# Two attention blocks on one core: A's V weights on another queue, their loads behind a VectorE copy, and the exps of phi(K) planned apart

## The chip, the cores and the metric

The kernel runs on one core of a Trainium2 chip. The core has five engines that run their own instruction streams and wait for each other on semaphores: TensorE (PE, matrix products into the PSUM banks), VectorE (DVE), ScalarE (ACT, exp and copies), GpSimd (POOL) and SyncE (SP, which only issues transfers). ACT and POOL issue transfers too, each on a queue of its own. The metric is the device time of one launch in microseconds; lower is better.

## The reference

Two independent blocks over 2048 positions and width 512, with 32 heads of 16; their results stand side by side in the output.

Block A (segments of 512 positions, with a memory that is carried along):

```python
phi = lambda t: where(t > 0, t + 1.0, exp(t))
for s in range(4):                      # segments of 512
    p = softmax(qs @ ks.T * scale + causal_mask)
    a_dot = p @ vs
    a_mem = (phi(qs) @ M) / (phi(qs) @ z + 1e-6)
    o = g * a_mem + (1 - g) * a_dot     # g = sigmoid(beta), one per head
    M += phi(ks).T @ vs;  z += phi(ks).sum()
out_a = concat(o) @ wo
```

Block B is plain attention of all 2048 queries over all 2048 keys, from one weight `wqkv`, followed by its own `wo`. All inputs are bf16.

## The kernel before

**Units.** The work is cut into units: one block of 512 queries and one group of four heads (`hg`, 0 to 7). A has 4 segments with 8 units each, B has 4 query blocks with 8 units each. The list begins with six units of A's first segment; from then on B's units stand, with A's others spread between them. For each unit PE makes scores with the keys on the partitions, ACT turns them into exps (L702 and L699 for A, L766 for B; called `pT`), and PE multiplies these with V into an accumulator `acc` (L924). A unit of A has five score tiles: widths of 1280 and 1024 alternate, and the last has 512. In A, POOL clears the masked triangle of each `pT` (L713) before PE may use it. B's exps are shared between ACT and DVE, which computes some of them with integer operations (L818, L784). A finished accumulator is transposed by DVE (L855), its row sums inverted (L858), and scaled by POOL (`rw` and `tN`, L872 and L876).

**Banks.** Scores lie in two tiles of PSUM, of three and two banks, used in turn. There are two further banks, `d_ps`, for everything else: projections (L334), DVE's scores (L807), memory and output products. There is one accumulator.

**Order.** The order of all instructions is written when the program is built, by a planner inside the kernel: a loop keeps a model time `c["t"]` and modelled times of ACT, DVE and POOL, and at each step issues scores, a batch of products with V, or a *chore*. A chore is a projection of K, Q or V, a transposition or an output product. Chores are sorted by due time and start once their condition holds, among others a model time at which their weights or inputs are taken to be there (`WA_AT`, `XB_AT`, `WB_AT`). `at(time, f)` puts an action off to a model time. On the chip each engine then runs its own instructions strictly in this order. Where the planner sees PE without work it puts filler products with zeros into the accumulator (L907).

**The front.** Four tiles of A's x and the first 128 columns of A's K and Q weights are loaded first (L75 to L78, SP and ACT). PE transposes x (L312); the halves are copied by ACT and by DVE (L953). Right behind ACT's copy stand, in the code, the loads of A's remaining weights (`load_rest_a`, L168 to L170). Then come the first Q and K projection, the two query masks by DVE (L963 and L967), B's loads on SP (`load_b`, L175 to L188), the K copy by ACT (L965) and the planner's loop. `setup_gates` (L143 to L154) makes the gates of A's memory, an exp on ACT, four small operations on DVE and ten on POOL. The later query tiles are masked by POOL (L353).

**phi(K).** For each of the four groups of 128 columns of A's K, SP transposes the finished keys (L399); later `more` (L401) makes exp on ACT into a tile `ek` that exists twice (L403), and three operations on POOL (L405 to L407). The time at which `more` is placed is not before `PHI_AT`.

Of the kernel before, what the change touches and what calls it, by code (L numbers as in the profile page):

```python
# [19 lines left out]
P = 128  # L20
# [21 lines left out]
def fast_path(ctx, tc, nc, A_x, A_wq, A_wk, A_wv, A_wo, A_beta, B_x, B_wqkv, B_wo, out, flag):  # L42
# [19 lines left out]
    def wview(w):  # L62
        return w.rearrange("(cc p) n -> p cc n", p=P)
    wq_a = const.tile([P, 4, D], BF16, name="wq_a")
    wk_a = const.tile([P, 4, D], BF16, name="wk_a")
    wv_a = const.tile([P, 4, D], BF16, name="wv_a")
# [18 lines left out]
    n = 1  # L85
# [41 lines left out]
    for j in range(4):  # L127
        nc.gpsimd.dma_start(out=beta_t[32 * j:32 * j + 32, :].rearrange("p (r t) -> p r t", t=2),
                            in_=bv[j].partition_broadcast(32))
# [35 lines left out]

    def load_rest_a():

        nc.scalar.dma_start(out=wv_a[:], in_=wview(A_wv))  # L168
        nc.scalar.dma_start(out=wk_a[:, :, P:], in_=wview(A_wk)[:, :, P:])
        nc.scalar.dma_start(out=wq_a[:, :, P:], in_=wview(A_wq)[:, :, P:])  # L170

# [15 lines left out]
        nc.sync.dma_start(out=wo_a[:], in_=wview(A_wo))  # L187
        nc.sync.dma_start(out=wo_b[:], in_=wview(B_wo))  # L188

    WA_AT = dict(v=6500, k=8500, q=10000)  # L190
    XB_AT, WB_AT = (10000, 18000, 23500, 28000), dict(k=13500, v=16000, q=21000)
    PHI_AT = 31000


# [37 lines left out]
    c = dict(t=0.0, act=0.0, dve=0.0, gp=0.0, mode=None)  # L232
# [37 lines left out]
    def act_cost(n):  # L270
        return 100.0 + 0.833 * n
# [8 lines left out]
    def gp_do(n, ready, rate=1.05):  # L280
        c["gp"] = max(c["gp"], ready) + 100.0 + rate * n
        return c["gp"]

    def act_do(ns, ready):
        c["act"] = max(c["act"], ready) + ns
        return c["act"]
# [4 lines left out]
    def at(time, fn):  # L291
        lcount[0] += 1
        heapq.heappush(later, (time, lcount[0], fn))
# [11 lines left out]
    def d_bank(dtype=F32):  # L305
        bank = d_next.pop() if d_next else ps_d.tile([P, 512], F32, name="d_ps", tag="d")
        return bank[:] if dtype == F32 else bank[:].bitcast(dtype)

    def fill_xT(bank, sbs):
        for n, i in enumerate(sbs):  # L310
            for cc in range(4):
                nc.tensor.transpose(bank[:, (4 * n + cc) * P:(4 * n + cc + 1) * P],  # L312
                                    xtiles[i][:, cc * P:(cc + 1) * P], ident[:])
        pe(60.0 * 4 * len(sbs), "full")
# [81 lines left out]
    def phi_k(s, rt):  # L396

        kn = phik_t[(s, rt)] = sb_.tile([P, 4, P], BF16, name="phik", tag="xin", bufs=4)
        nc.sync.dma_start_transpose(out=kn[:], in_=KT_at[(s, rt)][:])  # L399

        def more():  # L401
            e = sb_.tile([P, 4, P], BF16, name="ek", tag="e", bufs=2)
            nc.scalar.activation(e[:], kn[:], ACT.Exp)  # L403
            act_do(act_cost(512) + 100, c["t"])
            nc.gpsimd.tensor_scalar(e[:], e[:], 1.0, 0.0, ALU.min, ALU.max)  # L405
            nc.gpsimd.tensor_scalar(kn[:], kn[:], 3e38, 0.0, ALU.min, ALU.max)
            nc.gpsimd.tensor_tensor(kn[:], kn[:], e[:], op=ALU.add)  # L407
            gp_do(1024, c["act"] + LAT)
            gp_do(512, 0, 2.1)
            phik_at[s] = c["gp"] + LAT  # L410
            phik_n[s] = phik_n.get(s, 0) + 1
        at(max(c["dve"] + 12000, PHI_AT), more)

    def chore_k(k, s, rt):
        def evac(bank):
            uses(k, s)
            nc.vector.tensor_copy(k_dst(k, s, rt), bank)
            d_done(dve_do(dve_cost(512), c["t"] + LAT))
            k_ready[(k, s, rt)] = c["dve"] + LAT
            if k == "a" and s < NSEG - 1:  # L420
                phi_k(s, rt)
        d_job(lambda b, ccs: proj(b, ccs, weights(k, "k"), rsl(rt), xT_tile(k, s)), evac)
# [15 lines left out]
    def chore_q(k, s, rt):  # L438
        def evac(bank):
            uses(k, s)  # L440
            qc = sb_.tile([P, 512], BF16, name="qc", tag="qc", bufs=3)
            if k == "a":
                nc.vector.tensor_copy(qc[:], bank)
            else:
                nc.vector.tensor_scalar(qc[:], bank, QSCALE, None, ALU.mult)  # L445
            d_done(dve_do(dve_cost(512), c["t"] + LAT))
            q_masks(k, s, rt, qc)
            if k == "a" and s > 0:
                at(c["dve"] + 400, lambda: phi_q(s, rt, qc))
        d_job(lambda b, ccs: proj(b, ccs, weights(k, "q"), rsl(rt), xT_tile(k, s)), evac)  # L450
# [5 lines left out]
    def chore_v(k, i):  # L456
        def evac(bank):
            uses(k, i // 4)
            nc.vector.tensor_copy(v_dst(k, i), bank.rearrange("p (h d) -> p h d", d=DH))
            d_done(dve_do(dve_cost(512), c["t"] + LAT))  # L460
            v_ready[(k, i)] = c["dve"] + LAT
        d_job(lambda b, ccs: proj(b, ccs, weights(k, "v"), slice(0, D), xT_tile(k, i // 4), i % 4), evac)
# [79 lines left out]
    def chore(need, fn, ok=None, due=None, am=None):  # L542
        chores.append(dict(due=due, need=need, fn=fn, ok=ok, n=len(chores), am=am))

    def q_free(k, cc, rt):

        g = 4 * cc + rt - QTB[k]
        return g < 0 or exhausted(U[uidx[(k, g // 4, 2 * (g % 4) + 1)]])
# [5 lines left out]
    def begin(k, cc, hg):  # L554
        return U[uidx[(k, cc, hg)]]["at"]
# [5 lines left out]
    for i in range(4):  # L561
        chore(begin("a", 0, 0) + 4000 + 500 * i, lambda i=i: chore_v("a", i), ok=lambda: scount[0] >= 5 and now() >= WA_AT["v"])
    for rt in range(1, 4):
        n = begin("a", 0, 2 * rt)
        chore(n - 3000, lambda rt=rt: chore_k("a", 0, rt), ok=lambda rt=rt: now() >= WA_AT["k"] and q_free("a", 0, rt))
        chore(n - 4500, lambda rt=rt: chore_q("a", 0, rt), ok=lambda rt=rt: now() >= WA_AT["q"] and q_free("a", 0, rt))
    for g in range(4):
        n = b0 + 5500 * g
# [5 lines left out]
    for rt in range(1, 4):  # L574
        n = begin("b", 0, 2 * rt)
# [7 lines left out]
    for s in range(1, NSEG):  # L583
        n = begin("a", s, 0)
# [22 lines left out]
    n = 1e18  # L607
    for x in chores[::-1]:
        n = x["due"] = min(x["need"], n - (1200 if x["need"] < b0 + 35000 else 2500))
# [45 lines left out]
    def s_tile(dtype=F32):  # L655
        n = scount[0] % 2
        scount[0] += 1
        c["t"] = max(c["t"], sfree[n])
        return n, ps_s.tile([P, SCAP[n], 512 if dtype == F32 else 1024], dtype, name=f"s{n}_ps", tag=f"s{n}")
# [290 lines left out]
    for n in range(2):  # L950
        bank = d_bank(BF16)
        fill_xT(bank, (2 * n, 2 * n + 1))
        (nc.scalar.copy if n == 0 else nc.vector.tensor_copy)(  # L953
            xt0.rearrange("p c (i s) -> p i c s", s=P)[:, 2 * n:2 * n + 2], bank.rearrange("p (n c s) -> p n c s", n=2, c=4))
        if n == 0:
            load_rest_a()
    (_, pq), (_, pk) = s_tile(), s_tile()
    warm_up(2)
    proj(pq[:, 0, :], range(4), wq_a[:], rsl(0), xt0)
# [12 lines left out]
    for u in U[:2]:  # L972
        u["ready"] = t0 + 300
    at(t0 + 9000, setup_gates)
    at(t0 + 6000, lambda: phi_k(0, 0))


# [43 lines left out]
    while True:  # L1021
# [33 lines left out]
        if au is not None:  # L1055
            n = scount[0] % 2
# [518 lines left out]
@with_exitstack  # L1575
def kernel(
    ctx: ExitStack,
    tc: tile.TileContext,
    A_x: bass.AP,
    A_wq: bass.AP,  # L1580
    A_wk: bass.AP,
    A_wv: bass.AP,
    A_wo: bass.AP,
    A_beta: bass.AP,
    B_x: bass.AP,
    B_wqkv: bass.AP,
    B_wo: bass.AP,
    out: bass.AP,
):
    nc = tc.nc  # L1590
    args = (A_x, A_wq, A_wk, A_wv, A_wo, A_beta, B_x, B_wqkv, B_wo, out)
    top = ctx.enter_context(tc.tile_pool(name="top", bufs=1))
    flag = top.tile([P, 1], I32, name="flag")
    with tc.manual_schedule():
        fast_path(tc, nc, *args, flag)
    bad = nc.values_load(flag[0:1, 0:1], min_val=0, max_val=1)
    with tc.If(bad > 0):
        general_path(tc, nc, *args)
# [30 lines left out]
```

## Time and profile before

| | us |
|---|---|
| median of 6 runs | 905.63 |
| lowest and highest | 903.07 and 908.84 |
| the profiled execution | 906.15 |
| its span, first to last instruction | 904.4 |
| ACT busy | 841.4 (93%) |
| PE, DVE, POOL busy | 793.8 (88%), 786.9 (87%), 390.0 (43%) |
| issue to landing of A's V weights (ACT's queue) | 8.4 |
| the same for the rest of K's and of Q's weights | 9.1 and 9.8 |
| mean granted PE clock | 0.983 |

A line of the timeline has the start, the length, engine, source line, operation, the tiles written and read, and how many instructions it stands for (instructions of a row of them overlap a little); in brackets is the time for which the engine stood idle before, and what ended that. A line of a stretch has from:to, its length, busy time and count for PE, weight loads, DVE, ACT and POOL, and then the clock granted to PE (1.00 is full), the share of the transfer engines and GB/s. A busy time of PE contains what a slower clock adds.

### The profile page before, as it was taken

The numbers are of one execution on the slowest core, as the hardware profiler recorded it, in microseconds if no ns is written. First come the engines' busy times: TensorE is split into PE (matmuls) and PEld (weight loads), VectorE is DVE, ScalarE is ACT, GpSimd is POOL, SyncE is SP. The second block draws the span as 40 slices with busy tenths as digits, with TensorE's granted clock in tenths as the row PEclk, the third lists the DMA queues.
The fourth block names the chain that finished last, engine by engine and source line by source line (L and its number), as shares of the span: only waits on it lengthen the run. The fifth ranks groups of instructions, "written<-read, shape, count | busy, mean of one in ns | idle before, by whom it ended". The sixth has DMA issues, their size and how long they took to land.

```text
span 904.4 us, 24540 instructions
## 1 busy us (share of the span) xinstructions
PE 793.8 (88%) x10207; PEld 276.1 (31%) x10207; DVE 786.9 (87%) x1596; ACT 841.4 (93%) x786; POOL 390.0 (43%) x779
## 2 busy tenths in 40 slices
PE   7999889988899988898889988889988988988895
PEld 3323233332333323332223323322322332223232
DVE  4536888899999899979999999997899898999984
ACT  5689999999999999999999999999999998999993
POOL 5944424365342245634441555424441642354330
PEclk9989999999999999999999999999999998999997
DMA  8701000000000020010000000100000000000000
GB/s 188 135 2 30 1 2 13 19 8 2 1 8 20 7 31 2 1 31 2 7 1 14 19 2 7 25 1 8 19 2 1 25 3 1 2 2 1 1 25 29
DMA packets 31802, 15.83 MB, mean 17 GB/s; under 512 B 22976, under 2 KB 31680, under 8 KB 31680
## 3 DMA queue, kind: packets, MB, share of 16 engines
q1 hardware_dynamic: 28864, 12.19, 6.3%
q10 hardware_dynamic: 2688, 1.97, 0.7%
q8 instruction: 81, 1.33, 0.6%
q14 instruction: 41, 0.34, 0.1%
q0 software_dynamic: 128, 0.00, 0.0%
HBM read 4.72 MB, written 4.19 MB: 10 GB/s over the span
## 4 chain that ended last, share of the span: by engine, by line
PE 28%; ACT 28%; DVE 27%; issue 10%; POOL 5%; DMA 1%; ACTq 0%; DVEq 0%; POOLq 0%
ACT pT L766 24%; DVE pD L818 11%; PE acc L924 10%; DVE pD L784 9%; PE d_ps L334 6%; PE s_ps L761 6%; ACT pT L702 3%; DVE tT L855 3%; PE d_ps L807 2%; PE s_ps L692 2%; POOL pT L713 2%; PE acc L907 1%; DMA wk_a<-in_A_wk_dram 1%; DVE RA L858 1%; POOL mbd L485 1%
## 5 line engine op out<-in xcount | busy, mean ns | idle before, releaser
L766 ACT ACTIVATE pT<-s_ps 128x1536 bf16<-128x1536 f32 (+2 forms) x596 | 675.0, 1246 | 27.3 <-PE d_ps L807 12.7
L818 DVE TENSOR_SCALAR pD<-d_ps 128x512 int16<-128x512 f32 x586 | 378.9, 674 | 20.3 <-PE d_ps L807 18.8
L761 PE MATMUL s_ps<-QT_b,KT_b 32*128 32x512 bf16 x1462 | 233.2, 387 | 53.4 <-ACT pT L766 46.2
L784 DVE TENSOR_SCALAR pD<-pD 128x1024 int16<-128x1024 int16 (+1 forms) x606 | 265.3, 480 | 0.5
L924 PE MATMUL acc<-pD,VD 128*32 128x512 f16 x1758 | 222.2, 386 | 4.5 <-DVE tT L855 4.0
L807 PE MATMUL d_ps<-QT_b,KT_b 32*128 32x512 bf16 x586 | 209.8, 383 | 17.5 <-DVE pD L818 12.1
L924 PE MATMUL acc<-pT,VP_b 128*32 128x512 bf16 x1462 | 221.6, 386 | 0.1
L713 POOL TENSOR_SCALAR_AFFINE_SELECT pT<-pT 128x512 bf16<-128x512 bf16 (+3 forms) x192 | 95.7, 517 | 189.3 <-ACT pT L702 178.3
L702 ACT ACTIVATE pT<-s_ps 128x1024 bf16<-128x1024 f32 (+1 forms) x128 | 138.5, 1145 | 12.2 <-PE s_ps L692 10.2
L761 PEld LDWEIGHTS <-KT_b 32*128 32x128 bf16 x1462 | 71.7, 91 | 244.9 <-issue 233.0
L907 PE MATMUL acc<-ident,zero 128*32 128x256 bf16 (+1 forms) x1700 | 99.6, 291 | 3.9 <-DVE tT L855 3.7
L924 PEld LDWEIGHTS <-VD 128*32 128x32 bf16 x1758 | 62.5, 96 | 71.2 <-issue 51.7
L635 POOL TENSOR_SCALAR VD<-VP_b 128x288 bf16<-128x288 bf16 x192 | 74.1, 386 | 13.5
L924 PEld LDWEIGHTS <-VP_b 128*32 128x32 bf16 x1462 | 60.8, 96 | 46.5 <-issue 30.1
L692 PE MATMUL s_ps<-QT_a,KT_a 32*128 32x384 bf16 (+3 forms) x512 | 57.0, 302 | 11.8 <-ACT pT L702 5.9
L907 PEld LDWEIGHTS <-zero 128*32 128x32 bf16 x1700 | 40.8, 95 | 84.0 <-issue 80.0
L855 DVE STREAM_TRANSPOSE tT<-acc 128x512 f32<-128x512 f32 x64 | 45.3, 708 | 23.9 <-PE acc L924 21.3
L876 POOL TENSOR_TENSOR tN<-tT,RA 128x256 bf16<-128x256 f32 x31 | 20.4, 657 | 76.2 <-DVE RA L858 76.1
L807 PEld LDWEIGHTS <-KT_b 32*128 32x128 bf16 x586 | 46.8, 91 | 12.6 <-issue 9.7
L924 PE MATMUL acc<-pT,VP_a 128*32 128x256 bf16 (+3 forms) x512 | 39.5, 309 | 2.7 <-POOL pT L713 2.1
L507 POOL TENSOR_TENSOR tM<-aT,r 128x256 f32<-128x256 f32 x24 | 15.6, 648 | 59.7 <-DVE r L504 59.4
L353 POOL TENSOR_SCALAR QT_b<-qc,mq 128x512 bf16<-128x512 bf16 x32 | 25.3, 802 | 34.9 <-DVE qc L445 34.7
(111 smaller groups left out, 622.6 us busy)
## 6 DMA issues: line engine op xcount, KB each, us to landing
out_dram<-osb SPq DMA_DIRECT2D x30, 128.0 KB, 1.7
wv_a<-in_A_wv_dram ACTq DMA_DIRECT2D x1, 512.0 KB, 8.4
wk_b<-in_B_wqkv_dram SPq DMA_DIRECT2D x1, 512.0 KB, 5.1
wv_b<-in_B_wqkv_dram SPq DMA_DIRECT2D x1, 512.0 KB, 6.0
wq_b<-in_B_wqkv_dram SPq DMA_DIRECT2D x1, 512.0 KB, 5.3
wo_a<-in_A_wo_dram SPq DMA_DIRECT2D x1, 512.0 KB, 4.5
wo_b<-in_B_wo_dram SPq DMA_DIRECT2D x1, 512.0 KB, 6.8
wk_a<-in_A_wk_dram ACTq DMA_DIRECT2D x1, 384.0 KB, 9.1
```

Of the source, the lines that this page charges most:

```text
L635: mul = lambda dst, src: nc.gpsimd.tensor_scalar(dst, src, EXP_C[k], 1.0, ALU.mult, ALU.mult)
L692: nc.tensor.matmul(pt[:, b, col:col + w], kt[32 * j:32 * j + 32, kbl * P:(kbl + 1) * P], q[32 * j:32 * j + 32, P * kbl:512], start=(r == 0 ...
L702: nc.scalar.activation(pT[:].rearrange("p b n -> p (b n)")[:, 0:n], pt[:].rearrange("p b n -> p (b n)")[:, 0:n], ACT.Exp, scale=0.25)
L713: nc.gpsimd.affine_select(out=blk, in_=blk, compare_op=ALU.is_ge, fill=0.0, base=0, pattern=[[0, e - b], [0, w // P], [1, P]], channel_mul ...
L761: nc.tensor.matmul(pt[:, b, :], KT_b[32 * j:32 * j + 32, u["rt"], kb * P:(kb + 1) * P], q[32 * j:32 * j + 32, :], start=True, stop=True, t ...
L766: nc.scalar.activation(pT[:, 0:n, :], pt[:, 0:n, :], ACT.Exp, scale=1.0 / (LOG2E * 1024.0))
L784: nc.vector.tensor_scalar(tile[:, k, 0:n, :], tile[:, 0, 0:n, :], EXP_D[k], None, ALU.add)
L807: nc.tensor.matmul(bank, KT_b[32 * j:32 * j + 32, u["rt"], kb * P:(kb + 1) * P], qslice(u)[32 * j:32 * j + 32, :], start=True, stop=True, ...
L818: nc.vector.tensor_scalar(pd[:, 0, n, :], bank, EXP_B, 0.0, ALU.add, ALU.max)
L855: nc.vector.transpose(tT[:].rearrange("p c d -> p (c d)"), u["acc"][:])
L907: nc.tensor.matmul(bank[32 * j:32 * j + 32, 0:w].rearrange("p (n q) -> p n q", q=P), zero[:, 0:32], ident[:].unsqueeze(1).to_broadcast([P, ...
L924: nc.tensor.matmul(u["acc"][32 * j:32 * j + 32, e["c0"]:512], e["lhsT"], e["rhs"], start=(j not in u["started"]), stop=False, tile_positio ...
```

## The change

Four edits:

- A's V weights are loaded from SP's queue instead of ACT's. K's and Q's remaining columns stay on ACT's.
- `load_rest_a` is called after both copies of x instead of between them, and begins with three memsets by DVE of one column each of the tiles that the loads write. Each load has to wait for its memset, and DVE runs the memsets behind its own copy of x.
- The model times at which weights and inputs are taken to be there are shifted: A's by 500 to 1000, B's by -1500 to +1500.
- The earliest model time of the phi(K) exps becomes `PHI_AT + 3500 * rt`, so that each of the four column groups `rt` has its own.

The planner's loop itself is as before; with the other model times it writes another order for the front of the program.

```diff
     def load_rest_a():
 
-        nc.scalar.dma_start(out=wv_a[:], in_=wview(A_wv))
+        for w in (wv_a[:, 0, 0:1], wk_a[:, 0, P:P + 1], wq_a[:, 0, P:P + 1]):
+            nc.vector.memset(w, 0.0)
+        nc.sync.dma_start(out=wv_a[:], in_=wview(A_wv))
         nc.scalar.dma_start(out=wk_a[:, :, P:], in_=wview(A_wk)[:, :, P:])
         nc.scalar.dma_start(out=wq_a[:, :, P:], in_=wview(A_wq)[:, :, P:])
...
-    WA_AT = dict(v=6500, k=8500, q=10000)
-    XB_AT, WB_AT = (10000, 18000, 23500, 28000), dict(k=13500, v=16000, q=21000)
+    WA_AT = dict(v=7500, k=9000, q=10500)
+    XB_AT, WB_AT = (11500, 19500, 24000, 27500), dict(k=13000, v=14500, q=21000)
     PHI_AT = 31000
...
-        at(max(c["dve"] + 12000, PHI_AT), more)
+        at(max(c["dve"] + 12000, PHI_AT + 3500 * rt), more)
...
-        if n == 0:
-            load_rest_a()
+    load_rest_a()
```

## The prediction

> **What bounds the kernel now.** First the page: its busy shares and its row of granted clock.
>
> ```profile
> PE 793.8 (88%) x10207; PEld 276.1 (31%) x10207; DVE 786.9 (87%) x1596; ACT 841.4 (93%) x786; POOL 390.0 (43%) x779
> ...
> PEclk9989999999999999999999999999999998999997
> ```
>
> ScalarE (ACT) is the fullest engine, so a microsecond in which it has nothing to do is a microsecond of the total unless something else is as full at that place. One slice of the clock row near the front (the third, 45 to 68 us) reads 8. The edit moves instructions only at the front: the changed program has the same instructions as this one plus three memsets of one column and four filler matmuls; ACT's order differs up to its 45th instruction or so and is the same for all 1666 after it, TensorE's (PE) differs in the first 860 of 19,852 matmuls, all issued before about 75 us. So I read the front alone. ACT's own timeline, 16 to 60 us (start, length, what; in brackets the idle time before and who ended it):
>
> ```profile
> 18.88 1.02 ACT L702 ACTIVATE pT<-s_ps 128x1024 bf16<-128x1024 f32 x1 [0.57 <-PE s_ps L692]
> ...
> 20.51 1.24 ACT L702 ACTIVATE pT<-s_ps 128x1280 bf16<-128x1280 f32 x1 [0.51 <-PE s_ps L692]
> ...
> 25.72 4.20 ACT L702 ACTIVATE pT<-s_ps 128x1280 bf16<-128x1280 f32 x4 [3.42 <-PE s_ps L692]
> ...
> 41.00 1.18 ACT L403 ACTIVATE ek<-phik 128x512 bf16<-128x512 bf16 x2
> 45.30 0.63 ACT L403 ACTIVATE ek<-phik 128x512 bf16<-128x512 bf16 x1 [3.11 <-POOL phik L407]
> ...
> 50.88 0.60 ACT L699 ACTIVATE pT<-s_ps 128x512 bf16<-128x512 f32 x1 [0.87 <-PE s_ps L692]
> 52.40 2.54 ACT L766 ACTIVATE pT<-s_ps 128x1536 bf16<-128x1536 f32 x2 [0.93 <-PE s_ps L761]
> 55.56 1.45 ACT L766 ACTIVATE pT<-s_ps 128x1536 bf16<-128x1536 f32 x1 [0.63 <-PE s_ps L761]
> ```
>
> Two holes stand out: 3.42 us before 25.72, and 3.11 us before 45.30, where the third exp of phi(K) waits because its buffer `ek` exists twice and GpSimd (POOL) is still using the first. After the second hole come four small ones (0.87, 0.93, 0.63, and 0.16 before 57.17). The stretches around it say why:
>
> ```profile
> 41.00:47.50 6.50, 4.15 (x77) 2.80 (x73) 3.13 (x6) 3.39 (x6) 6.01 (x10) 1.00 0.00 0
> 47.50:54.50 7.00, 6.84 (x60) 1.57 (x56) 2.08 (x3) 5.15 (x6) 6.39 (x12) 0.51 0.01 4
> 54.50:61.50 7.00, 7.00 (x103) 2.40 (x99) 3.74 (x6) 6.21 (x6) 0.92 (x2) 1.00 0.00 0
> ```
>
> (Busy PE, weight loads, DVE, ACT, POOL; then the clock.) While ACT waits, its score banks stay full, PE stands idle for 2.35 us, and for the next 7 us its clock is 0.51: PE is then busy all the time and ACT is fed late. The first hole is POOL's:
>
> ```profile
> 16.31 4.30 POOL L713 TENSOR_SCALAR_AFFINE_SELECT pT<-pT 128x384 bf16<-128x384 bf16 x9 [8.79 <-ACT pT L699]
> 20.57 0.22 POOL L152 TENSOR_TENSOR maskg<-jm,mq 128x16 f32<-128x16 f32 x1
> ...
> 23.59 0.89 POOL L713 TENSOR_SCALAR_AFFINE_SELECT pT<-pT 128x512 bf16<-128x512 bf16 x2
> 24.47 1.38 POOL L353 TENSOR_SCALAR QT_a<-qc,mq 128x512 bf16<-128x512 bf16 x2
> ```
>
> Its first select runs at 16.31, though the exp that it needs ended at 12.05; from there it is never idle for long, and unit 2's queries (L353) come after 9 selects, 10 gate products and 2 more selects.
>
> **The change, part by part.** I number A's score tiles T1 to T30 (five to a unit, six units) and B's B1, B2 and so on.
>
> *Loads, memsets and gate.* Added: three DVE memsets (0.06 us each by the one on `xT_b`), behind the copy that ends at 6.20 and ahead of a DVE instruction that starts at 7.65: hidden; 0.2 us if that cover were gone. Moved: three issues. V's weights now wait on SP, K's and Q's rest on ACT, until about 6.3; before they were issued at 4.67, 5.08 and 5.64. Behind SP's wait stands only the transposed load of B's x, which waits until 8.35 for DVE anyway. Behind ACT's two issues stands its K copy (9.73): the last issue took 2.61 us and ended at 8.25; pushed to 6.9 it ends between 7.5 and 9.5, so the copy loses nothing. V's weights landed 8.4 us after their issue; from 6.3 that is 14.7. Lower bound 11.4 (the 5.1 us of `wk_b`, equally large and first on SP's queue); upper bound 16.1 (9.8 us, as for the last of the three). [...] I take 13.9 to 14.7. In the new order V's first half-projection comes one tile later than before, behind T4's scores (free from 13.0) and twelve fillers (0.5), at about 13.85, so PE may wait up to 0.9 us there. The cover is POOL's late start: the chain over POOL to unit 2 (below) has 1.6 us of slack on the V, Q side. Cost 0; beyond 15.4 it costs microsecond for microsecond. Could the K weights' first block land earlier than 8.59, with nothing issued beside it? From 0 to 1.1 us (K's projection follows Q's, which ends at 7.6). It reaches the end only if POOL's first select follows its exp rather than being ready at a fixed moment; the trace can't tell: 0 to 1.1, I take 0.2 and leave it out of the sum.
>
> *Unit 2's queries.* POOL's new order puts the query masks directly behind the gate products, and DVE makes the gates before V's fourth copy. From 16.31: selects 4.3, gate products 0.22+1.05+0.22+1.05 (without the 0.61 that POOL waited for DVE), give 23.1; first mask 0.7, scores and semaphore 0.5: T11 starts at 24.3 instead of 25.72. Gain 1.4. Against it, T9 and T10 now stand behind two more projections (0.87 us each) and start at about 21.4 instead of 20.51, but end at 23.2, before T11 can start.
>
> *T11 to T25.* Same tiles, other chores between them. PE was busy 15.14 of the 15.3 us here, so gaps come from a 16-matmul chore (0.87 us) in front of a tile's scores. Following the new order with these lengths I get gaps of 0.55, 0.2, 0.5, 0.15 and 0.25 before T16, T18, T19, T21, T24: 1.65 against 0.27+0.60+0.30 = 1.17. Loss 0.5.
>
> *The phi(K) exps.* Their planned times go from all 31000 to 31000, 34500, 38000; in the program they stand before T26, after T28 and after B1. Same three exps (0.65), no buffer wait: POOL has finished with the first `ek` (0.61+0.61+1.15 and gaps, 2.6 us) before the third. Gain 3.1. Where does it go? POOL still owes the 7.8 us of phi(K) work, now with selects between. I follow POOL from 24.5 with 3.05 us of selects and 0.93 of `rw`, `tN` for a unit: it is through the selects of T26 to T28 at 45.6 and of T30 at 50.4. PE's matmuls with these tiles are due at 48.5 and 52.8, so POOL is hidden with 2.4 us to spare.
>
> *The clock.* With no hole PE doesn't stand idle and the slow stretch goes. The four small gaps (2.59) become about 0.9 (0.25 at T29, 0.55 at B1, 0.1 at B3). Gain 1.7. [...]
>
> Sum: 1.4 - 0.5 + 3.1 + 1.7 = 5.7. That lets ACT's tiles follow each other as closely as in the rows of four (4.20 us); laid end to end with their single lengths the same steps give B5 at 54.05 instead of 58.1, a gain of 4.1, because PE can't be quicker in between (over 10.8 to 75 it was busy 58.4 of 64.2 us). I take 4.6, below the middle, since a wait that I haven't seen can only add. Behind B5 both programs owe the same work in the same order, so the shift stays. On the profiled execution (906.15, span 904.4 and 1.75 around it) that is 901.6; it lies 0.5 above the median of 905.63, so **901.0** for the median.
>
> **The rivals.**
> 1. *POOL becomes the bound.* Nearly idle-free from 16.3 to 50.5, it may reach T29 and T30 over 2.4 us later than worked out; PE's in-order queue then waits at their matmuls ahead of B5's scores. POOL's own end moves only from 54.3 to 52.8: gain 1.5, 904.1. For it: POOL's L713, L353 and L876 fill the chain of waits between 21 and 45 us. Against: the 2.4.
> 2. *The slow clock isn't in every execution.* If usual runs have no slow stretch at 47.5, the gain is 4.6 - 1.7 = 2.9: 902.7.
> 3. *V's weights late, on the other side.* If they land at 19 instead of 14.7, PE stands idle at its queue's head from 13.9; T5 and all behind wait. Past the slack that is 19 - 15.4 = 3.6; the idle PE loses its clock, under the densest projections (2.6 as above); and the later start takes the gain of 1.4 at T11. Then 905.6 - 4.6 + 3.6 + 2.6 + 1.4 = 908.6. It decides from a landing at 16.2 on, where PE's wait reaches the 2.35 us that cost the clock: 0.8 + 2.6 + 1.4 is 4.8, and the gain is gone. Against: the upper bound 16.1, which is near.
> 4. *The exps don't come apart*, because ACT reaches them together: then only 1.4 - 0.5 is left, 904.7. The built order speaks against it.
>
> **How the numbers follow.** Forecast 0.48, rival 2 0.16, rival 1 0.17, rival 4 0.04, rival 3 0.15. About 0.3%, 2.7 us, is what a measurement of this kernel tells from no change, so faster means below 902.9. That holds nine tenths of the forecast's cases (0.43), also in a good case with the earlier start, 897.5, and 0.11 of rival 2: with 0.08 of the other cases of rivals 1 and 4, 0.62. Slower is two thirds of rival 3 and a rest of all others: 0.13. Same: 0.25. Range 897.5 to 906.5: below it the sum of all gains without the PE limit, above it most of rival 3.
>
> **What would show it.** Right: T11 near 24.3, the three exps at L403 with no wait on POOL, no 0.5 clock between 40 and 60 us, B5 near 54, and the same distance from there to the end. Wrong: PE waiting for `wv_a` beyond 15.4; PE's L924 waiting for POOL's L713 behind B2; a clock of 0.5 at 16 to 24; or a shift at B5 that is gone at the end.

## The result, and the profile after

The changed kernel's median is 901.58 us (20 runs, 898.66 to 904.14). The kernel before, run beside it and with all its earlier runs, has 907.29 (41 runs). The ratio is 0.9934, with a 95% interval of 0.992 to 0.9948: 6.0 us faster, between 4.7 and 7.3. The forecast for the median was 901.0, from a base of 905.63; as a difference it was 4.6. The spans of the two profiled executions are 904.4 and 899.3.

In the changed kernel the lines behind the loads have moved down by 2 (L702 is L704, L403 is L405, L713 is L715). First the page, its busy shares and its clock:

```profile
PE 790.7 (88%) x10211; PEld 277.6 (31%) x10211; DVE 786.5 (87%) x1599; ACT 841.0 (94%) x786; POOL 389.6 (43%) x779
...
PEclk9999999999999999999999998989999999999999
```

The third slice now reads 9; two 8s stand further on, where the clock fell at 554, 581 and 602 us. ACT's own timeline, 16 to 60 us:

```profile
19.64 0.20 ACT L143 ACTIVATE gcol<-beta_t 128x8 f32<-128x8 bf16 x1
22.29 1.24 ACT L704 ACTIVATE pT<-s_ps 128x1280 bf16<-128x1280 f32 x1 [2.45 <-PE s_ps L694]
...
24.74 4.20 ACT L704 ACTIVATE pT<-s_ps 128x1280 bf16<-128x1280 f32 x4 [0.72 <-PE s_ps L694]
...
40.13 0.66 ACT L405 ACTIVATE ek<-phik 128x512 bf16<-128x512 bf16 x1
40.75 3.07 ACT L704 ACTIVATE pT<-s_ps 128x1024 bf16<-128x1024 f32 x3
43.69 0.64 ACT L405 ACTIVATE ek<-phik 128x512 bf16<-128x512 bf16 x1
44.53 1.24 ACT L704 ACTIVATE pT<-s_ps 128x1280 bf16<-128x1280 f32 x1 [0.20 <-POOL phik L409]
...
47.86 0.62 ACT L405 ACTIVATE ek<-phik 128x512 bf16<-128x512 bf16 x1
48.38 5.68 ACT L768 ACTIVATE pT<-s_ps 128x1024 bf16<-128x1024 f32 x5
54.31 6.07 ACT L768 ACTIVATE pT<-s_ps 128x1536 bf16<-128x1536 f32 x5 [0.25 <-PE s_ps L763]
```

The three exps of phi(K) stand apart, and none waits. B's tiles follow each other in rows of five where there were gaps of 0.93 and 0.63. The same three stretches as before:

```profile
41.00:47.50 6.50, 6.50 (x114) 3.51 (x110) 4.04 (x8) 6.05 (x7) 6.09 (x11) 1.00 0.01 4
47.50:54.50 7.00, 7.00 (x103) 2.84 (x98) 4.32 (x7) 6.74 (x8) 6.37 (x11) 1.00 0.00 0
54.50:61.50 7.00, 7.00 (x102) 2.05 (x90) 2.53 (x5) 7.00 (x7) 0.00 (x0) 1.00 0.01 2
```

PE is busy throughout at the full clock, and ACT rises from 3.39 to 6.05 and from 5.15 to 6.74. POOL's timeline, 16 to 25 us:

```profile
16.18 4.28 POOL L715 TENSOR_SCALAR_AFFINE_SELECT pT<-pT 128x384 bf16<-128x384 bf16 x9 [8.67 <-ACT pT L701]
20.42 0.23 POOL L152 TENSOR_TENSOR maskg<-jm,mq 128x16 f32<-128x16 f32 x1
21.28 1.05 POOL L154 TENSOR_TENSOR maskg<-jm,mqg 128x64 f32<-128x64 f32 x4 [0.64 <-DVE mqg L148]
...
23.49 1.38 POOL L355 TENSOR_SCALAR QT_a<-qc,mq 128x512 bf16<-128x512 bf16 x2
```

Unit 2's query masks (L355) follow the gate products directly, at 23.49 instead of 24.47.

Where the time came from is seen from each tile's start, before minus after: 0.98 at T11, 0.88 at T25, 5.08 at T26, 5.89 at B1, 6.40 at B5. From the 39th tile (63 us) to the 461st (549 us) it stays between 5.91 and 5.95. Behind that it moves where one kernel has a slow stretch of PE's clock that the other doesn't have there: 3.17 at tile 481, 1.90 at 601, 5.47 at the last. ACT's last 748 of 786 instructions have the same order in both traces.

### The profile page after: what moved, and what is told of

Its sections match the earlier page's. It is cut to its first block, busy times and chain, and to the rows that moved or that the text cites. A ratio compares the mean times of both kernels' runs of the same rounds, so it can differ in the third digit from the quotient of the medians.

```text
span 899.3 us, 24553 instructions
## 1 busy us (share of the span) xinstructions
PE 790.7 (88%) x10211; PEld 277.6 (31%) x10211; DVE 786.5 (87%) x1599; ACT 841.0 (94%) x786; POOL 389.6 (43%) x779
## 4 chain that ended last, share of the span: by engine, by line
PE 30%; ACT 28%; DVE 26%; issue 11%; POOL 3%; DMA 1%; ACTq 0%; DVEq 0%
ACT pT L768 26%; DVE pD L820 11%; PE acc L926 10%; DVE pD L786 9%; PE d_ps L336 8%; PE s_ps L763 6%; PE s_ps L694 3%; DVE tT L857 2%; PE d_ps L809 2%; ACT pT L704 2%; PE acc L909 1%; DMA wv_a<-in_A_wv_dram 1%; POOL pT L715 1%; DVE RA L860 1%; POOL mbd L487 1%
## 5 line engine op out<-in xcount | busy, mean ns | idle before, releaser
L715 POOL TENSOR_SCALAR_AFFINE_SELECT pT<-pT 128x512 bf16<-128x512 bf16 (+3 forms) x192 | 95.6, 517 | 187.8 <-ACT pT L704 177.0
L704 ACT ACTIVATE pT<-s_ps 128x1024 bf16<-128x1024 f32 (+1 forms) x128 | 138.6, 1146 | 12.9 <-PE s_ps L694 9.8
L355 POOL TENSOR_SCALAR QT_b<-qc,mq 128x512 bf16<-128x512 bf16 x32 | 24.9, 790 | 36.6 <-DVE qc L447 36.4
```

The costliest lines, as they stand in the source:

```text
L704: nc.scalar.activation(pT[:].rearrange("p b n -> p (b n)")[:, 0:n], pt[:].rearrange("p b n -> p (b n)")[:, 0:n], ACT.Exp, scale=0.25)
L715: nc.gpsimd.affine_select(out=blk, in_=blk, compare_op=ALU.is_ge, fill=0.0, base=0, pattern=[[0, e - b], [0, w // P], [1, P]], channel_mul ...
```

## The experiments

This table holds the traces of all kernels below (us on each trace's own axis). "Select to T11" runs from POOL's first masking select to T11. My own reckoning of the trace, used when I wrote the expectations, had T11 of before at 26.0; on the profile's axis it is 25.72, and only differences count.

| kernel | T1 | first mask select | T11 | select to T11 | T11 to T25 | T25 to tile 60 |
|---|---|---|---|---|---|---|
| before | 10.81 | 16.31 | 25.72 | 9.41 | 14.81 | 45.75 |
| b_again | 11.12 | 15.52 | 24.96 | 9.45 | 14.78 | 44.35 |
| b_phi | 9.55 | 17.41 | 26.96 | 9.55 | 14.80 | 40.66 |
| b_ek3 | 10.03 | 16.48 | 25.89 | 9.41 | 14.80 | 41.21 |
| b_fill | 9.47 | 17.44 | 27.91 | 10.47 | 14.77 | 42.93 |
| b_loads | 9.45 | 17.26 | 26.66 | 9.40 | 14.80 | 42.93 |
| b_times | 12.03 | 15.94 | 24.54 | 8.60 | 14.88 | 42.53 |
| a_nophi | 10.82 | 15.87 | 23.79 | 7.92 | 14.89 | 42.53 |
| after | 10.12 | 16.18 | 24.74 | 8.56 | 14.91 | 40.71 |
| a_again | 9.53 | 17.03 | 24.81 | 7.78 | 14.89 | 40.69 |
| a_early | 9.97 | 19.92 | 28.35 | 8.43 | 14.70 | 40.69 |
| a_gates | 14.51 | 19.49 | 29.18 | 9.69 | 14.30 | 40.68 |
| a_vfirst | 10.03 | 21.98 | 33.79 | 11.81 | 14.30 | 40.71 |
| a_nogate | 9.65 | 17.26 | 25.72 | 8.46 | 14.66 | 40.69 |

In b_times and a_nophi the planner wrote another order to the end of the program, so for these two the last column doesn't span quite the same work; the other columns do, as in the changed kernel.

The theory is the sum of the prediction: a hole in ACT's work that the phi(K) exps made, PE's slow clock behind it, and an earlier T11. The rivals are that the hole or the clock is worth something else, or that the loads or the order of the front bring the gain.

### The phi(K) exps alone

```diff
-        at(max(c["dve"] + 12000, PHI_AT), more)
+        at(max(c["dve"] + 12000, PHI_AT + 3500 * rt), more)
```

> The kernel before with one edit: the exps of phi(K) not before 31000 + 3500 * rt. By my theory this is the larger half of the change: T11 stays at 26.0 us, ACT has no wait on POOL at L403, the clock stays at 1.00 between 40 and 60 us, and from B's fifth tile on everything is about 5.0 us earlier than before (3.1 of waiting and some 1.7 to 2 of clock); time about 0.55% less. If the earlier loads and the other order up to T25 were what counts, it is within 1 us of before.

Measured: 903.57 against 906.44, ratio 0.9967 (0.995 to 0.9985), so 3.0 us (1.4 to 4.5). ACT's timeline, 39 to 56 us:

```profile
42.23 0.66 ACT L403 ACTIVATE ek<-phik 128x512 bf16<-128x512 bf16 x1
...
45.68 0.69 ACT L403 ACTIVATE ek<-phik 128x512 bf16<-128x512 bf16 x1
...
49.72 0.62 ACT L403 ACTIVATE ek<-phik 128x512 bf16<-128x512 bf16 x1
```

The hole is gone, and T25 to tile 60 falls from 45.75 to 40.66, the value of the whole change (40.71). By the medians this one line brings about half of the measured gain; the 5.0 that I had expected lies outside the interval.

### The same hole, closed by a third buffer

```diff
-            e = sb_.tile([P, 4, P], BF16, name="ek", tag="e", bufs=2)
+            e = sb_.tile([P, 4, P], BF16, name="ek", tag="osb" if (s, rt) == (0, 2) else "e", bufs=2)
```

> The kernel before, its exps where they were, but the third has a buffer of its own. If the wait for the buffer is all that costs, the three exps run back to back, the hole of 3.1 us and the slow clock go, and B's tiles are 4.8 us earlier. If POOL's order counts too: the three products (7.8 us) still stand ahead of the selects of T26 to T28, PE waits for these at about 53.0 us, some 1.5 us, and 3.3 us are left.

Measured: 901.92 (9 runs), ratio 0.9974 (0.9955 to 0.9993), so 2.4 us (0.6 to 4.1; the plain medians lie 4.5 apart). ACT's timeline, 39 to 60 us:

```profile
41.17 1.70 ACT L403 ACTIVATE ek<-phik 128x512 bf16<-128x512 bf16 x3
...
48.08 3.71 ACT L766 ACTIVATE pT<-s_ps 128x1536 bf16<-128x1536 f32 x3 [0.30 <-POOL phik L407]
52.45 8.14 ACT L766 ACTIVATE pT<-s_ps 128x1024 bf16<-128x1024 f32 x7 [0.65 <-PE s_ps L761]
```

With the exps still side by side but a buffer for each, ACT doesn't wait. The buffer was what it waited for, not the time of the exps as such. At 41.21 it is 0.5 worse than setting them apart: B1 and B4 come 0.30 and 0.65 late, which fits POOL's three triples of operations now standing in one piece ahead of the selects; that cause wasn't tried alone. PE itself waits for a select of POOL only once between 40 and 60 us, 0.16 at 53.92, not the 1.5 that I had put against this kernel.

### PE kept busy in the hole

Ten rounds of four products with zeros, in PE's order ahead of T28's scores (40 of them; they open the next unit's accumulator and add zeros to it):

```diff
+        if scount[0] == 29:
+            v = U[pvi[0]]
...
+            v["acc"] = ps_a.tile([P, 512], F32, name="acc", tag="acc")
+            for r in range(FILL_N):
+                for j in range(4):
+                    nc.tensor.matmul(v["acc"][32 * j:32 * j + 32, :].rearrange("p (n q) -> p n q", q=P), zero[:, 0:32],
+                                    ident[:].unsqueeze(1).to_broadcast([P, 4, P]), start=r == 0, stop=False,
+                                    tile_position=(0, 32 * j), skip_group_check=True)
+            v["started"] |= {0, 1, 2, 3}
```

> The kernel before, with 40 filler products with zeros put into PE's order at the 2.35 us in which it stood idle (ahead of T28's scores; they add nothing to the sums). The wait of 3.11 us stays. By my theory the clock then stays at 1.00, the four small gaps behind the hole (2.59 us) shrink to about 0.9, and B's tiles are 1.7 us earlier. If the gaps come from the backlog of projections and not from the clock, nothing moves or it is up to 1 us later.

Measured: 906.21, ratio 1.0002 (0.9984 to 1.0021): no gain. In its trace the hole is there (ACT's waits), PE is filled (its timeline), and the clock stays full (the stretch 47.5 to 54.5):

```profile
ACT ek L403 <- POOL phik L407: 3.1, 1, 3.1
```

```profile
46.90 2.34 PE L690 MATMUL acc<-ident,zero 128*32 128x512 bf16 x40 [0.20 <-DVE tT L865]
```

```profile
47.50:54.50 7.00, 6.93 (x110) 2.44 (x99) 2.25 (x4) 6.92 (x8) 6.40 (x10) 1.00 0.02 4
```

T25 to tile 60 is 42.93 instead of 45.75. So the slow clock cost 2.82 us in the trace of before, and the bare hole 42.93 - 40.69 = 2.24. But the median didn't fall: a slow clock in every execution, worth 1.7 as I had it, lies just outside the interval (1.5 faster to 1.9 slower). The next run bears on that.

### The loads alone

The load part of the change (V on SP's queue, three memsets, the call behind both copies), the order of the work as before.

```diff
-        nc.scalar.dma_start(out=wv_a[:], in_=wview(A_wv))
+        for w in (wv_a[:, 0, 0:1], wk_a[:, 0, P:P + 1], wq_a[:, 0, P:P + 1]):
+            nc.vector.memset(w, 0.0)
+        nc.sync.dma_start(out=wv_a[:], in_=wview(A_wv))
...
-        if n == 0:
-            load_rest_a()
+    load_rest_a()
```

> The kernel before with the load part alone (V's weights on SP's queue, all three behind DVE's copy and memsets, model times as before). By my theory the K weights' first block lands up to 0.7 us earlier and the first exp starts at 10.1 to 10.4, but POOL's first select stays at 16.2 to 16.3 and T11 at 26.0, so B's tiles move by less than 0.2 us. If the front's start sets the rest, all is 0.7 us earlier; if V's weights come too late for their old place at 13.1, PE waits about 1 us there and all is later by that.

Measured: 906.14, ratio 1.0003 (0.9984 to 1.0022): no gain seen. Select to T11 is 9.40 as before, though K's first projection starts at 7.21 instead of 8.63. And this trace has the full hole without the slow clock (ACT's timeline, then the stretch):

```profile
46.23 0.63 ACT L405 ACTIVATE ek<-phik 128x512 bf16<-128x512 bf16 x1 [3.11 <-POOL phik L409]
```

```profile
47.50:54.50 7.00, 6.49 (x95) 2.26 (x95) 2.77 (x4) 6.92 (x8) 6.49 (x11) 1.00 0.01 4
```

Nothing filled PE here, and T25 to tile 60 is 42.93 again. So the clock fell behind this hole in the execution of before (0.51 from 47.5 to 54.5) and not in this one (1.00).

### Both kernels once more

> The kernel before once more, for its profile: whether the clock of 0.5 behind the hole of 3.11 us comes in every execution (T60 45.7 us behind T25) or not (42.9), and where POOL's first select and T11 lie (expected 16.2 to 17.5, and 9.7 us behind it).

> The changed kernel once more, for its profile: T60 40.7 us behind T25 as in its first one, T11 8.9 us behind POOL's first select; the clock of 0.5 at 14.8 us and those behind 500 us may be elsewhere or missing.

Measured: spans 907.6 and 903.8. In b_again the slow stretch is 3.41 us long instead of 6.83, and T25 to tile 60 is 44.35. Three executions with an unfilled hole thus give a clock cost of 2.82, 1.42 and 0, mean 1.4; that is a mean of three, just inside the interval of b_fill. In a_again the lead over the first trace of before is 5.88 us at tile 60, and 0.90 at the end: slow stretches at 242, 321, 437 and 539 us take it. So the time of one execution says little about an edit of this size; the tile starts near the edit and the medians do.

### The model times alone, and the change without the phi(K) part

In b_times the two lines with `WA_AT`, `XB_AT` and `WB_AT` of the change, and nothing else; in a_nophi the change with

```diff
-        at(max(c["dve"] + 12000, PHI_AT + 3500 * rt), more)
+        at(max(c["dve"] + 12000, PHI_AT), more)
```

> The kernel before with the model times of weights and inputs of the changed one, loads and phi(K) exps as before. PE's and POOL's order up to T25 is then the changed one. If the order alone makes the front's gain, T11 stands 8.9 us behind POOL's first select and the ratio is that of loads and times together; if the loads' new place is needed too (V's weights landing before PE asks for them), PE waits longer for them here and the ratio is nearer to 1.000.

> The changed kernel with the exps of phi(K) back at one time (31000), so loads and model times alone. My prediction's sum gives it 0.9 us (1.4 for T11, less 0.5): about 905.5, and by ratio 0.999. If before usually loses more at its front than its profile showed (PE idle at V's weights and a clock of 0.5 from 13 us on, as in two of the runs with before's order), it is 2 to 3 us faster than before; T11 then at 25.0 to 25.5 with POOL's first select at 16.2 to 17.4 and T11 8.9 us behind that.

Measured: b_times 903.59, ratio 0.996 (0.9945 to 0.9975); a_nophi 902.65, ratio 0.9962 (0.9946 to 0.9978). Both gain more than the 0.9 that I had for the front. Select to T11 is 8.60 and 7.92 instead of 9.41, as the new order should give. The rest is not the front. With the new times the planner set the third exp two tiles behind the others, though the code asks for the same time (ACT's waits of b_times):

```profile
ACT ek L403 <- POOL phik L407: 1.0, 1, 1.0
```

It waits 1.0 instead of 3.1 (0.99 in a_nophi), and the clock stays full in both traces between 40 and 60 us. So a part of what the hole cost goes with these times too, and the two edits are not independent. The medians can't show that: the parts alone, 3.0 and 3.6, against the whole, 6.0, are equal within intervals of some 1.5 us either way.

Nor are the medians of these two kernels a measure of the front. Without the phi(K) line the planner's order differs from that of before and of the changed kernel to the end: ACT has 758 score tiles instead of 756, the first of another width is the 55th, and the mean granted clock of the runs is 0.990, against 0.983 for before and 0.986 for the changed kernel. How much of the 3.6 and 3.4 us comes from behind the front these runs don't say. What the phi(K) line is worth on top of the rest is therefore read from T25 to the 50th tile, up to which all have done the same work but for fillers: 31.34 in a_nophi, 29.71 in after, so 1.6 us.

### What sets POOL's first select

The prediction left open whether it follows its exp or is ready at a fixed moment. In the changed kernel, beta's four loads are moved to the front of POOL's order, and behind them stands a select on a tile that nothing reads:

```diff
-    seg_v(0)
...
+    first = const.tile([P, P], BF16, name="first")
+    nc.gpsimd.memset(first[:], 0.0)
+    nc.gpsimd.affine_select(out=first[:], in_=first[:], compare_op=ALU.is_ge, fill=0.0, base=0,
+                            pattern=[[1, P]], channel_multiplier=-1)
+    seg_v(0)
```

> The changed kernel, with two steps of GpSimd's start in another order: its four loads of beta are issued first, and directly behind them stands one select on a tile of its own (a tile of zeros that nothing reads), so that whatever a first select has to fetch starts near 3 us instead of 7.5. TensorE's and ScalarE's order is that of the changed kernel. Theory F (the first select of the masks is ready at a fixed moment after GpSimd's first instruction of that kind, 8.7 to 9.9 us, whatever its exp does): the first L713 starts within 1 us of its exp's end, at 11.5 to 13 instead of 16.2, GpSimd then waits for VectorE's gates, and T11 comes at 23.8 to 24.7 instead of 24.7; the total gains 0 to 1 us on the changed kernel. Rival (the select follows its exp by some 4 us, or the wait is for something else): the first L713 stays at 15.5 to 17.4 and T11 at 24.7.

Measured: 905.56, ratio 0.9977 (0.9949 to 1.0005), 3.9 us slower than the change. POOL's timeline, 0 to 30 us:

```profile
3.90 0.22 POOL L129 MEMSET first<- 128x128 bf16 x1
15.84 0.28 POOL L130 TENSOR_SCALAR_AFFINE_SELECT first<-first 128x128 bf16<-128x128 bf16 x1 [11.72 <-issue]
16.09 0.40 POOL L115 MEMSET VP_a<- 128x64 bf16 x4
...
19.92 4.18 POOL L719 TENSOR_SCALAR_AFFINE_SELECT pT<-pT 128x384 bf16<-128x384 bf16 x9
```

The dummy needs only the tile cleared at 3.90, and POOL stands at it from 4.12. It runs at 15.84. Theory F falls: the moment doesn't move with the time at which POOL reaches its first select (4.1 or 7.5), nor with T1: in the eleven traces of the table whose masks come first it runs at 15.52 to 17.44, with T1 at 9.45 to 12.03, and the two earliest selects stand behind T1 at 11.12 and 10.82, the two latest behind 9.47 and 9.55. What it waits for the traces don't show, and I leave it open. My kernel also had a flaw: POOL's memsets for V and for two other tiles now stood behind the dummy, so the masks came 3.75 us later than in after. That makes it a test of another kind: T11 is 3.6 later, tile 60 3.4, the median 3.9. The delay at POOL's first mask goes to the end nearly in full here.

### Gates earlier, V first, no gate

a_gates is a_early with the gates planned at 3500 instead of 9000; a_vfirst is a_gates with V's load issued ungated right behind the first block of Q's weights:

```diff
-    at(t0 + 9000, setup_gates)
+    at(t0 + 3500, setup_gates)
```

```diff
     nc.sync.dma_start(out=wq_a[:, :, 0:P], in_=wview(A_wq)[:, :, 0:P])
+    nc.sync.dma_start(out=wv_a[:], in_=wview(A_wv))
...
-        nc.sync.dma_start(out=wv_a[:], in_=wview(A_wv))
```

> The kernel with the early select, and the planned time of the gates 3500 instead of 9000 ns behind its start: the gates' exp comes after T3 instead of after T6, and GpSimd's gate products with it. If GpSimd's late start with the gates behind it is what holds unit 2's queries, T11 comes at 23.2 to 24.0 (then set by the projection of unit 2's queries, which ends near 21.6, a copy and a mask of 0.7 each, and 0.5), 0.7 to 1.5 us ahead of the changed kernel, and all behind moves with it: total 0.7 to 1.5 us below the changed kernel, ratio to the kernel before 0.991 to 0.9925. Rival: PE's projections, not GpSimd, set T11, which stays at 24.5 or above, and the total is that of the changed kernel. Against a gain speaks also that ScalarE's in-order queue would wait for beta, should it land after 11 us.

> The kernel with early gates, with V's weights issued without a gate on SyncE's queue directly behind the first block of Q's weights (near 2.5 us); only the rest of K's and Q's weights stay gated. If the gate of the change costs what its trace shows, PE's wait of 0.94 us for V's weights (landing at 14.06) and the clock of 0.5 at 14.8 go: V lands by 10 to 11, V's first projection waits for nothing, T9 comes 1 us earlier, and the total 0 to 1 us below the kernel with early gates. Against it: 512 KB beside the first blocks, which the first scores wait for; if they share the DMA engines, K's projection starts 1 us or more later than the 7.3 to 7.9 of the changed kernel, and T1 with it, and the total is the same or up to 1 us worse.

Measured: 907.94 and 909.01, ratios 1.0007 (0.9988 to 1.0026) and 1.0015 (0.9996 to 1.0034), both slower than the change by 7 us. Both expectations missed, and both kernels carry the flaw of a_early. PE's waits of a_vfirst, 6 to 40 us, show it at work:

```profile
PE acc L930 <- POOL pT L719: 7.4, 2, 6.0
```

(In the trace of a_gates PE also waits 3.8 for Q's first block.) They don't answer what earlier gates would bring. Nor did V come early: issued at 2.18, its weights landed at 12.93. For the delay at POOL's first mask they are two further points: tile 60 is 3.8 and 8.4 later than after, the medians 6.6 and 7.3 by the ratios. That agrees in direction and rough size, not one for one.

In a_nogate the change stands without its gate: no memsets, the loads called behind the first copy as before.

> The changed kernel without the three memsets, and with the loads called for behind the first copy as before: V's weights on SyncE's queue and the rest on ScalarE's, without the gate; the order of all other work is that of the changed kernel. If the gate matters, K's first block lands 0.5 to 1.1 us later than with it (K's projection at 8.6 instead of 7.9) and T1 with it, while V's weights land 1 to 2 us earlier (12 to 13) and PE doesn't wait for them; both together leave T11 within 0.5 us of 24.7 and the total within 0.5 us of the changed kernel. If the gate is what the front part gains by, T11 comes 0.7 us later or more and the total by as much.

Measured: 903.7, ratio 0.9959 (0.9937 to 0.998), 2.3 us behind the change, with intervals that overlap. The issue of V's load waited for nothing on SP's queue, which makes this a test of an early V too:

```profile
2.18 0.51 SPq L168 DMA_DIRECT2D wv_a<-in_A_wv_dram  x1
```

In its trace K's first projection starts at 7.47, against 7.94 and 7.30 with the gate, and V lands at 12.93, the same as in a_vfirst, and inside the 11.92 to 14.05 of the six traces with the gate, which issued it between 5.73 and 6.26. Select to T11 is 8.46. T11 is 1.0 later than in after, about as the first select is (17.26 against 16.18). So neither the gate nor an issue without it brings K's first block or V clearly earlier here. Whether the gate brings 2 us in some other way these runs don't settle; the mean granted clock of the runs differs as well, 0.983 against 0.986.

## Why the prediction was right

- *The hole.* The exps came apart, before T26, after T28 and after B1, with no wait: shown by b_phi, and by b_ek3 as to the buffer. Its term of 3.1 was too large: the bare hole is worth 2.24, since the tiles behind it follow with no wait of note in b_fill (none is listed from 47.5 to 64 us), where the kernel without the hole waits 0.20, 0.26 and 0.25.
- *The clock.* The term of 1.7 was taken from one row. It measured 2.82, 1.42 and 0 in three executions; the mean is 1.4. Rival 2 is thus half true: the slow stretch came in two of the three (before and b_again) and not in b_loads. The last section has the rows at the hole for all three.
- *T11.* The order did what it should, 1.4 predicted: 0.98 in the profile. Where the rest went is in POOL's timeline: the wait of 0.64 for DVE's gates, which I had taken as gone. Behind it stands the first step, the loads. V's weights landed at 14.05, within the bounds, and PE waited as worked out:

```profile
PE d_ps L336 <- DMA wv_a<-in_A_wv_dram: 0.9, 1, 0.9
```

  But I costed that wait at nothing. PE's clock then fell to half (0.50 granted) for 3.41 us at 14.5, T6 to T8 came 1.9 us later behind T1 than in a_again, and the gates' exp, behind T8 on ACT, at 19.64 instead of 17.6 (a_early). This is rival 3 in small. In a_again and a_nophi, with V in time, select to T11 is 7.78 and 7.92. The mean of four traces with the change's order of the front (after, a_again, a_nophi, a_nogate) is 8.18, against 9.44 of the five with the old one: 1.26 for a predicted 1.4. (b_fill, where PE waited 2.3 for V, is left out; with it the old order has 9.62. So is b_times, the new order with the old loads, 8.60.)
- *The earlier start of K*, left out at 0 to 1.1: worth nothing. T11 keeps its distance to the first select, and that doesn't follow T1.
- *T11 to T25*, predicted 0.5 lost: 14.91 against 14.81, so 0.1.
- *POOL hidden*, rival 1: right. It was through the selects of T26 to T28 at 45.80 (45.6 predicted) and of T30 at 50.76 (50.4); PE waited for neither. Rival 4 is out by the timeline.
- *The discount.* B5 was put near 54 and came at 51.7. The sum of 5.7 would have given 52.4; I had cut it to 4.6, because PE had been busy for 58.4 of 64.2 us. That step failed: the 58.4 contained the stretch at half clock. The same tiles in the changed kernel took 58.97 us with PE busy for 56.44.
- *The same distance from there to the end*: to 0.04 us over 486 us (63 to 549), then blurred by slow stretches that both kernels have. The prediction's counts of 1666 and 19,852 take in a branch of the program that wasn't run: the traces have 786 instructions on ACT and 10,207 products on PE. What it read from them, that the order behind the front is the same, holds.

Averaged over executions the terms are 1.26 + 2.24 + 1.4 - 0.1 = 4.8. The measured 6.0 (4.7 to 7.3) holds that, near its edge; what makes the other 1.2, if it is more than chance, stays open. So the forecast of 4.6 was right in size, but partly by luck: hole and clock, 1.2 too large together, were undone by the needless cut of 1.1.

## What to carry to other kernels

An engine that waits for a buffer still in use by a slower one can be helped by moving the producer's instruction as well as by another buffer: here T25 to tile 60 fell from 45.75 (42.93 where the clock stayed full) to 40.66 by the one and to 41.21 by the other. Price the wait by the distance between two tiles far on either side, not by its own length: the wait of 3.11 was worth 2.24. When you count a busy PE as a bound, take the stretches of slow clock out of the count first: the 58.4 us of before held 6.83 at half clock, and the changed kernel was busy for 56.44 with the same tiles. And a delay at the head of an engine's queue can reach the end nearly in full, as 3.75 us at POOL's first mask came to 3.4 at tile 60, so ask what the first instruction of each engine waits for before reordering anything ahead of it.

## What the runs showed of the hardware that I had not expected

**PE's clock fell to half in short stretches.** In the trace of before it is granted at 0.50 for 6.83 us each from 47.67, 583.56 and 750.81, for 3.41 from 883.93, and from 897.59 to the end; in that of after for 3.41 us each from 14.49 and 601.58, for 6.83 from 553.80 and 581.10, and from 895.13 to the end. One hole came with 2.82, 1.42 and 0 us of slow clock in three executions. Here are its rows in before and in b_again, the 3.41 us ahead of the fall and what follows, and two rows of that length around the hole in b_loads, where the clock stayed full, each from its own trace:

```profile
44.26:47.67 3.41, 1.06 (x17) 0.32 (x12) 1.22 (x3) 2.37 (x3) 3.16 (x4) 1.00 0.00 0
47.67:51.08 3.41, 3.25 (x31) 0.92 (x31) 1.27 (x2) 2.54 (x4) 3.16 (x6) 0.50 0.01 2
51.08:54.50 3.42, 3.42 (x29) 0.65 (x25) 0.81 (x2) 2.43 (x3) 3.06 (x7) 0.50 0.02 5
```

```profile
43.65:47.06 3.41, 1.03 (x13) 0.41 (x13) 1.05 (x3) 2.56 (x4) 3.16 (x4) 1.00 0.00 0
47.06:50.48 3.42, 3.26 (x31) 0.82 (x30) 1.38 (x2) 2.55 (x4) 3.17 (x6) 0.50 0.01 2
50.48:53.89 3.41, 3.41 (x56) 1.11 (x52) 1.39 (x2) 2.88 (x4) 2.85 (x7) 1.00 0.02 5
```

```profile
43.90:47.31 3.41, 1.58 (x30) 1.03 (x22) 2.44 (x5) 1.08 (x2) 3.08 (x5) 1.00 0.00 0
47.31:50.73 3.42, 2.72 (x43) 0.98 (x42) 1.04 (x2) 3.42 (x4) 3.09 (x5) 1.00 0.01 2
```

PE stands idle for the same 2.35 us in each. In before and b_again the 3.41 us ahead of the fall hold 1.06 and 1.03 us of work. In b_loads the hole lies across the two rows, with 1.58 and 2.72 us; but the 3.41 us that end with its hole, at 47.83, hold no more than 3.41 - 2.35 = 1.06 either, and the clock stayed at 1.00. So the idle time alone doesn't tell the executions apart. Nor is a single limit on busy time in the traces: the 3.41 us ahead of the stretch at 14.5 in after had 2.07 us of it, part of it products with zeros, and yet the clock fell. What decides it stays open, and so does why the slow stretch lasted 6.83 us in before and 3.41 in b_again, with 3.25 and 3.26 us of work in the first 3.41 of each.

**POOL's first select ran at 15.52 to 17.44 us** in the eleven traces whose masks come first, with POOL free for it from 7.51 in after, and at 15.84 in a_early, with POOL free from 4.12. For a_early the trace names no transfer or engine that released it, after 11.72 us of idle time.

**One load, many landings.** V's weights, 512 KB, landed 5.7 us after their issue in b_loads, 6.1 in a_again and 8.3 in after, all three on SP's queue behind the same gate. Issued about 4 us earlier without the gate, in a_vfirst and a_nogate, they took 10.8 us.
